# Other layout and other steps for the stacks, the maxima and the loads of an attention kernel, and an output projection of 14 products

## The chip, the cores and the metric

One core of a Trainium2 chip runs the whole kernel. The metric is the device time of one execution in microseconds; three executions of the kernel before took 717.62, 720.45 and 721.08 us, median 720.45. Less is better. The core has five engines with queues of their own that work in order: TensorE (PE, with its weight loads as PEld), VectorE (DVE), ScalarE (ACT), GpSimd (POOL) and SyncE (SP), which here only issues transfers (DMA). The profile's lines are those of the kernel before.

## What is computed

Two parts that share nothing are computed and set side by side: `a`, an attention with memory, and `b`, a filter in the frequency domain.

```python
# a: S=2048 rows, D=576, H=32 heads of 18, N=4 segments of 512 rows
for s in range(4):
    logits = qs @ ks.T * scale + mask          # causal, within the segment
    a_dot  = softmax(logits) @ vs
    a_mem  = (phi(qs) @ M) / (phi(qs) @ z + 1e-6)     # phi(t): t+1 if t>0, else exp(t)
    o      = g * a_mem + (1 - g) * a_dot       # g = sigmoid(beta), one per head
    M += phi(ks).T @ vs;  z += phi(ks).sum()
a = concat(o) @ wo
# b:
b = irfft2(rfft2(x) * (w_r + 1j * w_i))
```

## The kernel before, in words

Everything is kept near float32 by splitting: a float32 number becomes two (`fp32r`) or three (`bf16`) parts, and a product becomes a sum of products of parts.

The time line has four stages. First the forward transform of `b` (`FFT.forward`). Then the projections (`ATT.projections`): for each of four segments nine tiles of 128 columns of Q and K (`qk_unit`, four of Q, one that is half Q and half K, four of K) and four of V (`v_unit`), with the middle of the transform taken in between. Each tile of Q and K is split into three bf16 parts (`sp3`) and stored in DRAM (`qkD`); phi of Q is stored too (`pqD`), phi of K is transposed on TensorE (`ptr`) and copied to `pk` for the memory. Third comes the inverse transform, into which `prologue` weaves the start of attention. Last comes attention proper, a loop over `t` with one head of one segment per step, 128 heads and 5 steps to run out.

The work is in order by hand (`manual_schedule`): generators emit instructions, and the loop in `attention` says which generator goes on at which place of a step. `hh` is `t` modulo 4, a group `k` has four heads, a stack `n` has two groups. In step `t`:

- `s1(t+10)` computes the scores of the head ten ahead, in three accumulations, and takes their row maxima on DVE. For two of the three (`red`) DVE adds the causal mask itself (L641, then a read of its accumulator); in the other the mask comes by a product with a triangle (`tri`, L646).
- `mpath(k+2)` turns four heads' maxima into rows of the stack Q: it gathers them (L659, L660), splits them in two on GpSimd (`mh`, L662, L663), transposes them on TensorE (L666), copies them (`mts`, L669), and two steps later ACT's queue sends them into rows 108 and 109 of Q (L672). It begins at `hh==1` and goes on at `hh==3`.
- `s2(t)` computes the transposed scores with the maxima already subtracted (L682 to L691, 110 rows: 108 of the stack and 2 of the maxima) and ACT takes the exponentials; at `hh==3` GpSimd cuts the triangles of four heads (L696).
- `pv` multiplies with V (L711), `pv_out` and `u_dmas` store the result (`U`, `uD`, `rD`).
- `run_bg(1.2)` advances the background by 1.2 steps per head: `mixed`, which combines segment `g-1` (`combine`: `ux` and `pb` to `am`, then the parts `oh` and `ol`, L819 and L832) and begins the memory term of segment `g` (`mem1`); `den`, the denominators of the next segment (L765, it reads `pq`, which `mem1` loads); and `oproj`, the output projection of segment `g-1` (L849).
- Transfers wait in lists `q` and `qu` and are issued two per step on SP's queue; `later(k, f)` puts one some steps off.

A stack has 108 rows of 8 heads by 512: six pairs of bf16 parts of Q and K by 18 numbers of a head. `stack_dmas` loads it in six transfers of 18 rows; each row is gathered from eight pieces of 1 KB, since `qkD` has one row per column of the weights with three parts of 1 KB behind one another. Stacks for Q are three in turn, for K four.

`oproj` has for each of four blocks of 128 rows and two halves of 288 columns an accumulation of 15 products: five tiles of rows (four of 126, one of 72) times three pairs of parts (`oh` with `woh`, `oh` with `wol`, `ol` with `woh`). The last segment goes through `last_proj` instead.

Of the kernel before, what the change touches and what calls it, by code (L numbers as in the profile page):

```python
# [340 lines left out]
BF=mybir.dt.bfloat16  # L341
H=32; DH=18; SC=float(DH)**-0.5
# [41 lines left out]
class ATT:  # L384
    def __init__(s,nc,tc,io,cp,dp):
# [6 lines left out]
        s.qkD=[d(f"qkD{i}",[1152,3,512],BF) for i in range(4)]  # L392
# [68 lines left out]
    def qk_unit(s,g,mt,tp,pp):  # L461
# [9 lines left out]
        nc.scalar.copy(sp3[:,0],ps)  # L471
# [6 lines left out]
        nc.vector.tensor_tensor(ps,ps,sp3[:,0],op=OP.subtract)  # L478
# [3 lines left out]
        nc.scalar.copy(sp3[:,1],ps)  # L482
        yield
        nc.tensor.matmul(ps,s.nid,sp3[:,1],start=False,stop=True,skip_group_check=True)
        nc.scalar.copy(sp3[:,2],ps)
        nc.sync.dma_start(s.qkD[g][128*mt:128*mt+128],sp3)
# [3 lines left out]
        n=r1-k0; c0=128*mt+k0-576  # L490
# [4 lines left out]
        nc.scalar.copy(s.pk[:,:,c0:c0+n],pt[:,:,:n])  # L495
# [99 lines left out]
    def late_setup(s,cp):  # L595
# [3 lines left out]
        s.woh=cp.tile([126,5,576],F32R,name="woh",bufs=1); s.wol=cp.tile([126,5,576],F32R,name="wol",bufs=1)  # L599
        for t in range(6):  # L600
            if t>1: yield
            if t<5:
                x=cp.tile([128,576],F32,name="ob")[:126]; q.append(x)
                nc.sync.dma_start(x,io["wo"][:,576*t:576*t+576])
            for _ in range(2): yield
            if t>0:
                x=q.pop(0)
                nc.scalar.copy(s.woh[:,t-1],x)
                nc.gpsimd.tensor_tensor(s.wol[:,t-1],x,s.woh[:,t-1].bitcast(F32),op=OP.subtract)
        yield  # L610
        yield from s.gates()
    def stack_dmas(s,n,qk):

        nc=s.nc; g,G=divmod(n,4)
        L=[]
        T,base,order=((s.Qs[n%3],0,(0,0,0,1,1,2)),(s.Ks[n%4],576,(0,1,2,0,1,0)))[qk]
        for pc,o in enumerate(order):
            a=s.qkD[g][base+8*G*18:base+8*G*18+18,o]
            ap=bass.AP(tensor=a.tensor,offset=a.offset,ap=[[1536,18],[1536*18,8],[1,512]])
            def go(T=T,pc=pc,ap=ap):  # L620
                nc.sync.dma_start(T[18*pc:18*pc+18],ap)
                if pc==5: s.loaded.add((n,qk))
            L.append(go)
        return L
# [5 lines left out]
    def s1(s,t):  # L630
# [163 lines left out]
    def mixed(s,g):  # L794
# [3 lines left out]
        for i in range(5+d):  # L798
            next(c,None); yield
            if i>=d:  # L800
                for _ in s.mem1(g,i-d): yield
# [4 lines left out]
    def combine(s,g):  # L806
# [6 lines left out]
        def high(u):  # L813
            r=126 if u<4 else 72
            s.oh[u]=tp.tile([126,512],F32R,name="oh",bufs=5); s.ol[u]=tp.tile([126,512],F32R,name="ol",bufs=5)
            (nc.vector.tensor_copy if s.now>=119 else nc.scalar.copy)(s.oh[u][:r],s.am[u][:r])
        def low(u):
            r=126 if u<4 else 72
            eng().tensor_tensor(s.ol[u][:r],s.am[u][:r],s.oh[u][:r].bitcast(F32),op=OP.subtract)  # L819
        late=g==2  # L820
        for t in range(7+late):
            if t>1 and not late: high(t-2); low(t-2)
            if t<5:
                r=126 if t<4 else 72; x=xs[t]
# [8 lines left out]
                if t<2: s.later(1,lambda t=t: s.ux_load(g,t+3))  # L833
            if late and 1<t<7: high(t-2)
            if late and t>2: low(t-3)
            yield
    def oproj(s,g):
        nc=s.nc
        oh,ol=s.oh,s.ol
        for tb in range(4):  # L840
            ob=s.tp.tile([128,576],F32,name="ob")
            c=slice(128*tb,128*tb+128)
            for hf in range(2):
                ps=(s.ps.tile([128,512],F32,name="po",tag=s.potag) if s.potag else s.post("po"))[:,:288]
                w=slice(288*hf,288*hf+288)
                L=[(a,b,t) for a,b in ((oh,s.woh),(oh,s.wol),(ol,s.woh)) for t in range(5)]
                for i,(a,b,t) in enumerate(L):
                    r=126 if t<4 else 72
                    nc.tensor.matmul(ps,a[t][:r,c],b[:r,t,w],start=i==0,stop=i==14)  # L849
                    if i==7: yield  # L850
# [41 lines left out]
    def prologue(s):  # L892
# [7 lines left out]
        for t in range(10):  # L900
# [223 lines left out]
```

## Time and profile before

| | before |
|---|---|
| three executions, us | 717.62, 720.45, 721.08 (median 720.45) |
| the profiled execution, us | 718.92 |
| its span, first to last instruction, us | 717.2 |
| granted TensorE clock, mean | 0.997 |
| instructions | 14460 |
| DMA packets, under 2 KB of them | 83304, 50750 |

The profile shows one execution. Busy time of an engine is the time in which it works on at least one instruction; a window counts it in a stretch of the span. A wait names the engine and line that waited, and what ended the wait. The chain follows back from the last instruction to whatever released each step. The attention loop runs from about 355 to 680 us, the projections from about 75 to 275 us, the inverse transform between them.

### The profile page before, as it was taken

To read this page: it belongs to the slowest core of one execution; us is meant where nothing else is said; L and a number is where in the kernel's file an instruction comes from. 1 tells how busy PE (TensorE), PEld (TensorE's weight loads), DVE (VectorE), ACT (ScalarE), POOL (GpSimd) and SP (SyncE) were. 2 spreads that over 40 slices of the span, in tenths; PEclk is the share of its full clock that TensorE was granted. 3 is DMA by queue.
4 is the path that set the end of the run, shared out by engine and by line. 5 is a ranking of instruction groups with operands and counts; after the bars stand their busy time and mean duration, and the time that the engine had idled before them with its cause. 6 is when DMAs were issued, how large, how long until landed. Compare 5 with 4: busy or idle time off the path is not lost. (4 is left out here: it accounts for less than half of the span.)

```text
span 717.2 us, 14460 instructions
## 1 busy us (share of the span) xinstructions
PE 684.1 (95%) x5007; PEld 505.7 (71%) x5007; DVE 552.3 (77%) x1270; ACT 450.1 (63%) x985; POOL 211.1 (29%) x403
## 2 busy tenths in 40 slices
PE   4999999999999999999999899899999999999997
PEld 4988869879779879999854444444466445664497
DVE  5999979899699789788588787878466876568633
ACT  3665796585586575444487677767466776567521
POOL 5432000100200111665154333435123662235300
PEclk9999999999999999999999999999999999999999
DMA  8995435645363568899547665776446775441152
GB/s 305 293 280 164 148 118 185 192 169 182 110 220 147 178 198 281 208 231 228 165 111 174 171 172 136 185 173 170 114 126 158 195 169 126 126 137 42 28 153 83
DMA packets 83304, 121.02 MB, mean 169 GB/s; under 512 B 11472, under 2 KB 50750, under 8 KB 83096
## 3 DMA queue, kind: packets, MB, share of 16 engines
q1 hardware_dynamic: 76580, 104.11, 50.3%
q0 software_dynamic: 5632, 15.76, 8.0%
q8 instruction: 39, 0.64, 0.4%
q10 hardware_dynamic: 1020, 0.25, 0.2%
q14 instruction: 33, 0.27, 0.1%
HBM read 81.78 MB, written 38.24 MB: 167 GB/s over the span
## 5 line engine op out<-in xcount | busy, mean ns | idle before, releaser
L641 DVE CUSTOM_DVE_ANT_0 junk<-s,x 128x512 bf16<-128x512 f32 (+1 forms) x256 | 141.4, 552 | 67.2 <-PE s L637 62.0
L696 POOL TENSOR_SCALAR_AFFINE_SELECT P<-P 128x512 f32<-128x512 f32 (+2 forms) x132 | 78.8, 623 | 67.3 <-ACT P L683 51.8
L647 DVE TENSOR_REDUCE mx<-s 128x4 f32<-128x512 f32 x128 | 87.7, 686 | 2.9 <-PE s L646 0.7
L683 ACT ACTIVATE P<-s 128x512 f32<-128x512 f32 x128 | 76.4, 597 | 16.5 <-PE s L682 5.4
L711 PE MATMUL pv<-P,vs 128*32 128x512 f32 (+3 forms) x1024 | 82.8, 441 | 0.0
L692 ACT ACTIVATE P<-s 128x256 f32<-128x256 f32 x128 | 49.4, 386 | 49.7 <-PE s L691 49.6
L688 ACT ACTIVATE P<-s 128x512 f32<-128x512 f32 x128 | 76.1, 594 | 2.0 <-PE s L687 1.8
L637 PE MATMUL s<-Ks,Qs 108*128 108x384 bf16 (+3 forms) x256 | 69.1, 301 | 1.2 <-DVE mx L647 0.9
L711 PEld LDWEIGHTS pv<-P,vs 128*32 128x32 f32 x1024 | 27.2, 109 | 45.3 <-issue 42.5
L459 PE MATMUL pj<-x,wqkh 128*128 128x512 f32 x162 | 56.5, 409 | 0.0
L205 DVE TENSOR_TENSOR Z<-t,t 128x290 f32<-128x290 f32 (+1 forms) x96 | 48.4, 554 | 0.1
L637 PEld LDWEIGHTS <-Qs 108*128 108x128 bf16 x320 | 31.5, 98 | 22.6 <-issue 11.3
L506 POOL MEMSET vt<- 128x32 f32 x16 | 2.4, 166 | 149.1 <-PE pm L516 127.7
L205 DVE TENSOR_TENSOR t<-Z 128x580 f32<-128x580 f32 x64 | 46.0, 755 | 0.0
L142 PE MATMUL f<-ftab,eh 128*128 128x290 f32 (+1 forms) x160 | 32.5, 322 | 12.1 <-DMA ftab<-ftab 9.5
L646 PE MATMUL s<-tri,idb 128*128 128x128 bf16 x256 | 43.2, 220 | 0.0
L295 PE MATMUL i<-civ,Y 128*128 128x256 f32 (+1 forms) x288 | 39.0, 288 | 0.2 <-POOL Y L280 0.2
L295 PEld LDWEIGHTS i<-civ,Y 128*128 128x128 f32 (+1 forms) x288 | 36.4, 181 | 1.0 <-POOL Y L280 0.4
L306 PE MATMUL i<-itab,T 128*128 128x290 f32 (+1 forms) x224 | 36.3, 305 | 0.1
L637 PE MATMUL s<-Ks,x 108*128 108x384 bf16 (+3 forms) x128 | 35.3, 306 | 1.1 <-DVE mx L647 0.6
L142 PEld LDWEIGHTS f<-ftab,eh 128*128 128x128 f32 (+1 forms) x160 | 26.2, 207 | 14.1 <-issue 8.5
L459 PE MATMUL pj<-x,wqkl 128*128 128x512 f32 x90 | 35.5, 395 | 0.0
(203 smaller groups left out, 1820.8 us busy)
## 6 DMA issues: line engine op xcount, KB each, us to landing
qkD<-sp SPq DMA_DIRECT2D x36, 384.0 KB
Ks<-qkD SPq DMA_DIRECT2D x72, 144.0 KB
x<-qkD SPq DMA_DIRECT2D x60, 144.0 KB
Qs<-qkD SPq DMA_DIRECT2D x60, 144.0 KB
xin<-xb SPq DMA_DIRECT2D x16, 384.0 KB
cfw<-cfw POOLq DMA_DIRECT2D x16, 384.0 KB, 4.4
civ<-civ POOLq DMA_DIRECT2D x16, 384.0 KB, 7.6
vs<-vD SPq DMA_DIRECT2D x16, 330.0 KB
```

The costliest lines, as they stand in the source:

```text
L142: nc.tensor.matmul(p[:,r,:FP],x,t,start=n==0,stop=n==6)
L205: v.tensor_tensor(o,a,b,op=op)
L295: nc.tensor.matmul(p[:m,k],Y[i][:,q,c*128:c*128+m],cc[:,hl,o:o+256],start=n==0,stop=n==5)
L459: s.nc.tensor.matmul(out,a,b,start=i==0,stop=i==len(L)-1)
L637: nc.tensor.matmul(out,Q[:108,h,128*i:128*i+128],K[:108,h,:128*(i+1)],start=True,stop=True)
L641: nc.vector.tensor_tensor_reduce(out=junk[:,:w],in0=src,in1=s.mask[:,512-w:],scale=1.0,scalar=-3.0e38, op0=OP.add,op1=OP.max,accum_out=s.m ...
L647: nc.vector.tensor_reduce(out=s.mx[k][:,hh],in_=pa.rearrange("p (b c) -> p b c",c=128),axis=mybir.AxisListType.X,op=OP.max)
L683: nc.scalar.activation(P[0][:,hh],p0,AF.Exp,scale=SC)
L688: nc.scalar.activation(P[1][:,hh],p1,AF.Exp,scale=SC)
L692: nc.scalar.activation(P[2][:,hh],p2,AF.Exp,scale=SC)
L696: nc.gpsimd.affine_select(out=x[:,r],in_=x[:,r],pattern=[[0,r.stop-r.start],[1,128]],compare_op=OP.is_ge,fill=0.0,base=0,channel_multiplie ...
L711: nc.tensor.matmul(s.pvt[32*hh:32*hh+32,128*j:],vt[:,j,19*h:19*h+32],mv[0][:,hh,mv[1]],start=j==0,stop=j>1,skip_group_check=True)
```

## The change

1. *Stacks.* The columns of the weights of Q and K are put in another order on the host: tiles 0 to 3 hold the first 16 numbers of 8 heads of Q each, the middle tile the last two numbers of all heads of Q and of K, tiles 5 to 8 those of K like Q. `qkD` gets one block per tile with the parts outermost, so that eight heads of one number and one part are 8 KB in a row; K's parts are stored in reversed order. The middle tile goes to `reD`, with parts repeated, in six stores. A stack is loaded by four transfers of 48, 32, 16 and 12 rows of 8 KB. `pqD` and `pk` keep their old order, so their stores and copies go by steps.
2. *Maxima.* `s1` works on the head eleven ahead (the prologue does one head more), and `mpath` begins at `hh==0` and goes on at `hh==1`. For heads 11 to 14 all three accumulations get the triangle by a product, and DVE a plain reduction.
3. *Loads and background.* The three loads of `ux` move into the wait of the reciprocals, three to five heads earlier. Four steps of `oproj` go ahead of `den`. The five tiles of a segment are taken in the order 4, 0, 1, 2, 3.
4. *Projection.* For segments 0 to 2 the fifth tile's three products become two: rows 72 to 127 of `oh` and rows 72 to 87 of `ol` for that tile are filled, by three transfers within SBUF, with copies of parts, and `woh` and `wol` get matching rows from a sixth load of `wo`.

```diff
+ORD=(4,0,1,2,3)
...
 def host_wo(w):
-    o=np.zeros((126,5,D),np.float32)
-    o[:,:4]=w[:504].reshape(4,126,D).transpose(1,0,2)
-    o[:72,4]=w[504:]
+    o=np.zeros((128,6,D),np.float32)
+    o[:126,:4]=w[:504].reshape(4,126,D).transpose(1,0,2)
+    o[:72,4]=w[504:]; o[72:,4]=w[504:560]; o[72:88,5]=w[560:]
...
-        s.qkD=[d(f"qkD{i}",[1152,3,512],BF) for i in range(4)]
+        s.qkD=[d(f"qkD{i}",[8,3,128,512],BF) for i in range(4)]
+        s.reD=[d(f"reD{i}",[24,32,512],BF) for i in range(4)]
...
-        if qr>r0: nc.sync.dma_start(s.pqD[g][128*mt:128*mt+qr],e[:qr])
+        if qr>r0:
+            a=s.pqD[g][0]
+            J=[(18*8*mt*512,[[512,16],[18*512,8]],e[:qr])] if mt<4 else [((16+j)*512,[[18*512,32]],e[32*j:32*j+32]) for j in range(2)]
+            for o,ap,x in J: nc.sync.dma_start(bass.AP(tensor=a.tensor,offset=a.offset+o,ap=ap+[[1,512]]),x)
...
-        nc.sync.dma_start(s.qkD[g][128*mt:128*mt+128],sp3)
+        if mt!=4: nc.sync.dma_start(s.qkD[g][mt-(mt>4)].rearrange("i p c -> p i c"),sp3)
+        else:
+            for r,i,c,n in ((0,0,1,3),(0,1,1,2),(0,2,1,1),(64,0,3,3),(64,0,2,2),(64,0,1,1)):
+                m={3:0,2:3,1:5}[n]; a=s.reD[g][r*12//64+2*m]
+                x=sp3[r:r+64,i:i+c] if c==n else sp3[r:r+64,i:i+1].to_broadcast([64,n,512])
+                nc.sync.dma_start(bass.AP(tensor=a.tensor,offset=a.offset,ap=[[512,64],[64*512,n],[1,512]]),x)
...
-        nc.scalar.copy(s.pk[:,:,c0:c0+n],pt[:,:,:n])
+        pk=s.pk.rearrange("p a (h d) -> p a h d",d=18)
+        if mt==4: nc.scalar.copy(pk[:,:,:,16:],pt[:,:,:n].rearrange("p a (d h) -> p a h d",d=2))
+        else: nc.scalar.copy(pk[:,:,8*mt-40:8*mt-32,:16],pt.rearrange("p a (d h) -> p a h d",h=8))
...
-        T,base,order=((s.Qs[n%3],0,(0,0,0,1,1,2)),(s.Ks[n%4],576,(0,1,2,0,1,0)))[qk]
-        for pc,o in enumerate(order):
-            a=s.qkD[g][base+8*G*18:base+8*G*18+18,o]
-            ap=bass.AP(tensor=a.tensor,offset=a.offset,ap=[[1536,18],[1536*18,8],[1,512]])
-            def go(T=T,pc=pc,ap=ap):
-                nc.sync.dma_start(T[18*pc:18*pc+18],ap)
...
+        T=(s.Qs[n%3],s.Ks[n%4])[qk]
+        u=G+4*qk
+        for p0,i0,i1 in ((0,0,3),(48,qk,2+qk),(80,2*qk,1+2*qk)):
+            L.append(lambda p0=p0,i0=i0,i1=i1: nc.sync.dma_start(T[p0:p0+16*(i1-i0)].rearrange("p a c -> p (a c)"),s.qkD[g][u,i0:i1].rearrange("i (d h) c -> (i d) (h c)",h=8)))
+        def go():
+            nc.sync.dma_start(T[96:108],s.reD[g][12*qk:12*qk+12,8*G:8*G+8])
...
+            if 11<=t<15:
+                nc.tensor.matmul(src[:,w-128:w],s.idb,s.tri,start=False,stop=True,skip_group_check=True)
+                nc.vector.tensor_reduce(out=s.mg[k][:,hh,i:i+1],in_=src,axis=mybir.AxisListType.X,op=OP.max)
+                return
...
+            A,B=s.oh[u],s.ol[u]
+            l=B if u<4 else tp.tile([128,512],F32R,name="ol4",bufs=1)
+            eng().tensor_tensor(l[:r],s.am[u][:r],A[:r].bitcast(F32),op=OP.subtract)
+            if u==4:
+                s.later(1,lambda: nc.sync.dma_start(B[:72].bitcast(F32),A[:72].bitcast(F32)))
+                s.later(2,lambda: (nc.sync.dma_start(A[72:128].bitcast(F32),l[:56].bitcast(F32)),nc.sync.dma_start(B[72:88].bitcast(F32),l[56:72].bitcast(F32))))
...
-                L=[(a,b,t) for a,b in ((oh,s.woh),(oh,s.wol),(ol,s.woh)) for t in range(5)]
...
+                L=[(a,b,t,126) for a,b in ((oh,s.woh),(oh,s.wol),(ol,s.woh)) for t in range(4)]+[(oh,s.woh,4,128),(ol,s.wol,4,88)]
...
-        for t in range(10):
+        for t in range(11):
...
+                        if 2<i<6: s.ux_load(g-1,ORD[i-3])
                         next(r); yield
-                    for u in range(3): s.ux_load(g-1,u)
                     yield from r
                     bg.append(s.mixed(g))
-                    if g<3: bg.append(s.den(g+1,lane))
-                    bg.append(s.oproj(g-1))
+                    o=s.oproj(g-1)
+                    if g<3: bg.append(itertools.islice(o,4)); bg.append(s.den(g+1,lane))
+                    bg.append(o)
...
-            a=s.s1(t+10) if t+10<128 else iter(())
+            a=s.s1(t+11) if t+11<128 else iter(())
...
-            if hh==3 and m is not None: steps(m,1)
+            if hh==1 and m is not None: steps(m,1)
             steps(b,1)
-            if hh==3 and m is not None: steps(m,1)
-            if hh==1 and k+2<32: m=s.mpath(k+2); next(m)
+            if hh==1 and m is not None: steps(m,1)
+            if hh==0 and k+2<32: m=s.mpath(k+2); next(m)
```

More of the change, by code (lines that the diff above doesn't have):

```diff
@@ L832, in combine @@
                     eng().tensor_tensor(s.am[t][:r],x[:r],s.am[t][:r],op=OP.add)
[L833 to L835 removed]
+                t=i
+                if t<2: s.later(1,lambda t=t: s.ux_load(g,ORD[t+3]))
+            if late and 1<t<7: high(ORD[t-2])
+            if late and t>2: low(ORD[t-3])
             yield
```

71 lines of the change are left out of this document (38 added, 33 removed).

## The prediction

> **What bounds the kernel now.** I read the page's busy times first, then the stage windows, then TensorE's waits in the attention stage, and the chain last. The page's first part, one profiled execution:
>
> ```profile
> PE 684.1 (95%) x5007; PEld 505.7 (71%) x5007; DVE 552.3 (77%) x1270; ACT 450.1 (63%) x985; POOL 211.1 (29%) x403
> ```
>
> TensorE is busy nearly throughout. Whether it is the limit is read per stage; three windows (columns: stretch, length, busy time of PE, weight load, DVE, ACT and POOL, granted clock, DMA share, GB/s):
>
> ```profile
> 140.00:180.00 40.00, 40.00 (x243) 34.55 (x242) 37.27 (x68) 28.57 (x57) 0.35 (x4) 1.00 0.57 190
> 300.00:340.00 40.00, 40.00 (x321) 37.53 (x320) 34.34 (x86) 17.61 (x44) 23.00 (x35) 1.00 0.92 228
> 415.50:423.50 8.00, 8.00 (x76) 4.14 (x74) 6.94 (x22) 6.13 (x17) 2.88 (x7) 1.00 0.68 183
> ```
>
> The projections (first), the inverse transform with its prologue (second) and four undisturbed heads of attention (third) leave TensorE no gap; DVE and ACT have one to two microseconds over in eight. So time is won by fewer products or shorter waits of TensorE, and lost by new waits of it. The waits there are, from 355 to 680 us (total us, times, longest):
>
> ```profile
> PE s L682 <- DMA Qs<-mts: 3.2, 3, 1.4
> PE pd L765 <- DMA pq<-pqD: 1.4, 1, 1.4
> PE pb L826 <- DMA rr<-rrD: 1.2, 1, 1.2
> PE s L637 <- DMA Qs<-qkD: 0.4, 1, 0.4
> PE s L682 <- DMA x<-mts: 0.2, 1, 0.2
> ```
>
> All five end on a transfer, 6.4 us together. The chain (start, length, what) tells how long these transfers take and what the products of the output projection cost:
>
> ```profile
> 372.67 7.55 DMA Qs<-mts
> ...
> 401.24 5.59 DMA x<-mts
> ...
> 458.87 0.68 SPq L805
> 459.61 0.38 SPq L805
> 460.03 0.48 SPq L805
> 460.61 5.79 DMA rr<-rrD
> 466.44 0.38 PE pb L826
> ...
> 481.35 8.42 DMA Qs<-mts
> ...
> 500.58 6.41 DMA pq<-pqD
> ...
> 512.28 1.25 PE po L849 x8
> ...
> 693.37 2.93 PE po L849 x22
> ```
>
> **Products of the output projection.** 22 products in 2.93 us are 0.133 us each. Segments 0 to 2 have 8 accumulations each (four blocks of rows, two halves); each loses one of 15: 24 x 0.133 = **-3.2 us**, all on the path, since TensorE is the limit there.
>
> **Maxima eleven heads ahead.** The transfer of the maxima (mts) was issued three heads before its first use, some 6 us at 8.00 us for four heads, and lands 5.6 to 8.4 us after issue (chain): hence the waits. It is issued two heads earlier now, five heads or 10 us ahead, more than the longest landing. Both mts rows go: **-3.4 us**. What is late next is the transposition of the maxima, which now follows their making by one head instead of two; TensorE takes its work in order, so it and all behind it would wait. One head's worth of rows in the undisturbed stretch:
>
> ```profile
> 415.04 0.63 POOL L696 TENSOR_SCALAR_AFFINE_SELECT P<-P 128x512 f32<-128x512 f32 x1
> ...
> 415.39 0.27 PE L637 MATMUL s<-x,Qs 108*128 108x256 bf16 x1
> ...
> 416.72 0.08 DVE L641 DVE_READ_ACCUMULATOR2_ANT mg<- 128x1 f32 x1
> ...
> 418.13 0.28 PE L637 MATMUL s<-x,Qs 108*128 108x256 bf16 x1
> ...
> 418.53 0.22 PE L646 MATMUL s<-tri,idb 128*128 128x128 bf16 x1
> ...
> 418.59 0.22 PE L637 MATMUL s<-Ks,Qs 108*128 108x128 bf16 x1
> ...
> 418.80 0.08 DVE L641 DVE_READ_ACCUMULATOR2_ANT mg<- 128x1 f32 x1
> ...
> 419.44 0.22 POOL L663 TENSOR_TENSOR mh<-mg,mh 128x16 bf16<-128x16 f32 x1
> ...
> 422.19 0.22 PE L666 MATMUL mt<-idb,mh 128*128 128x128 bf16 x1
> ```
>
> Before: the last maximum at 418.80, its two halves done on GpSimd at 419.66, 0.86 us later; transposed at 422.19, 2.5 us to spare. After: the last maximum of a group falls one head earlier, like that at 416.72, so the halves are done at 417.58, and TensorE asks for them right behind the product at 418.13: 0.7 us to spare. GpSimd also takes its work in order:
>
> ```profile
> L819 POOL TENSOR_TENSOR ol<-am,oh 126x512 fp32r<-126x512 f32 (+1 forms) x10 | 12.7, 1270 | 16.4 <-ACT oh L816 15.4 <-PE pn L784 1.0
> L832 POOL TENSOR_TENSOR am<-ux,am 126x512 f32<-126x512 f32 (+1 forms) x8 | 10.1, 1273 | 4.5 <-DVE ux L831 3.3 <-PE s L682 1.2
> ```
>
> Where one of these 18 stands in front, TensorE waits 1.27 - 0.7, about 0.6 us. A transposition comes in every fourth head, so some four or five are hit; the first one or two come while DVE is still catching up: **+1.5 us** for about 30 transpositions, ends 0 and 11 (18 x 0.6). I take the low part, because the combining steps that issue the 18 also lengthen TensorE's own heads. GpSimd's selects, the only other work of size there, end before that place (the last at 415.67). The other instructions of the step (a reduction on DVE, two small copies on ACT, the issue on ACT's queue) move along, their number unchanged; ACT has the time, as 6.13 of 8 us show.
>
> The eight accumulations of heads 11 to 14 that get the triangle by a product cost one product of 128 columns each, 0.06 us (418.53 to 418.59): **+0.5 us**; DVE saves its 0.08 us of reading the accumulator each time, which I count as nothing. The eleventh head in the prologue moves one head's score products from one stage bound by TensorE to another: 0.
>
> **Loads at other steps.** The three loads of ux stood on SP's queue right before rr (458.87 to 460.61, 1.7 us), and TensorE waited 1.2 us for rr. They go three to five heads earlier: **-1.2 us**; rr is then not late. Four steps of the output projection now stand between the last load of pq (issued at 500.58, landed 6.41 us later) and the denominators that read it. Each step holds seven products, four take over three heads, more than 6.4 us: **-1.4 us**. A window on each side of that wait (columns as above):
>
> ```profile
> 504.50:508.00 3.50, 2.08 (x13) 0.35 (x5) 1.26 (x3) 1.32 (x3) 0.41 (x2) 1.00 0.62 146
> 508.00:511.50 3.50, 3.50 (x19) 1.59 (x22) 1.82 (x5) 2.12 (x4) 0.83 (x2) 0.52 0.48 131
> ```
>
> After the window with the wait, the granted clock is 0.52 for 3.5 us: 3.5 x 0.48 = **-1.7 us** more, which go with the wait. [...]
>
> **Stacks.** Four transfers instead of six, on the page:
>
> ```profile
> Ks<-qkD SPq DMA_DIRECT2D x72, 144.0 KB
> Qs<-qkD SPq DMA_DIRECT2D x60, 144.0 KB
> ```
>
> The bytes stay, the issues fall from 192 to 128. A row of 8 KB isn't in this trace; its ends are the wait it could remove, **-0.4 us** (Qs<-qkD above), and the same wait again if it lands later. I take the first: fewer issues stand in front. Otherwise loads are hidden by a whole group's heads (16 us). If that cover went, each of 13 later Q stacks would show as the 0.4 did, +5 us.
>
> What pays for it lies in the projections: the store of qkD in pieces of 1 KB, five more stores for each middle tile, one more of pqD, columns of pk written in another order. All stores are SP's and nobody on TensorE waits for them within its 3.5 us per tile; no stack is read before the projections of segment 3, and then it is one of segment 0. The copy to pk reads PSUM in steps of eight elements. Nearest rows:
>
> ```profile
> L495 ACT COPY pk<-ptr x15: 357/588/622, 100.5 to 225.5; 128x512 f32<-128x512 f32 x12, 128x256 f32<-128x256 f32 x3
> PE pj L484 <- ACT sp L482: 1.9, 3, 1.0
> ```
>
> Between no change and the slowest elementwise row of that width (1.27 us, GpSimd above) it costs ACT 0 to 10 us in all; ACT has about 11 us over in 40 there, but in segment 0 TensorE already waits for ACT (second row, 1.0 us at most). So 0 on the path, with up to 3.4 us (five copies x 0.68) as upper end.
>
> The three copies from SBUF to SBUF per segment make SP wait for GpSimd's 1.27 us; behind them stand stack loads with heads to spare. They are read by the last two products of an accumulation, some 46 us after the combining begins (466.44 to 512.28): 0, and if that cover went, a landing of 6 to 8 us, once per segment. That the tile of 72 rows is combined first changes no count: 0. The sixth load and copy of wo fall in segment 0, on ACT: 0.
>
> **Sum.** -3.2 - 3.4 + 1.5 + 0.5 - 1.2 - 1.4 - 1.7 - 0.4 = **-9.3 us**. The profiled execution took 718.92 us (span 717.2), so 709.6 by its own time. It is 1.5 us faster than the median of the three runs, 720.45; from that median it is **711.1 us**.
>
> **Rivals.**
> 1. *The transposition becomes the wait (slower).* If GpSimd's selects slip behind the making of the maxima, so that a 1.27 us operation or two selects of 0.63 stand in front every time, each of 30 transpositions costs 0.6 us or more; at 0.5 us each the 15 us eat the gain (10.8 without its own term) and more, at 0.8 us it is 720.45 - 10.8 + 24 = 734. For it: only 0.7 us to spare. Against it: GpSimd is busy 2.88 of 8 us. Deciding point against half a percent: 14.4/30 = 0.48 us.
> 2. *The waits turn up elsewhere (no change).* ACT (6.13) and DVE (6.94 of 8.00) use the pauses to catch up; without them TensorE waits for them instead. Only the products count: 720.45 - 3.2 + 0.5 = 717.8. For it: DVE's 87%. Against it: the undisturbed stretch runs at full pace.
> 3. *The maxima still land late.* Rows of 8 KB ahead of small pieces lengthen their landing beyond 10 us: 711.1 + 3.4 = 714.5. The longest landing seen is 8.42.
> 4. *The strided copy delays the projections*: 711.1 + 3.4 = 714.5. [...]
> 5. *More waits go* (those of DVE at the start of attention, of ACT on earlier mts transfers): up to 6 us more, 705.
>
> **How the numbers follow.** Forecast 0.55, rival 1 0.08, rival 2 0.11, rival 3 0.10, rival 4 0.08, rival 5 0.08. Half a percent, 3.6 us, is what a measurement tells from no change: below 716.8 is faster. Faster 0.81 (forecast and rivals 3, 4, 5), same 0.11 (rival 2), slower 0.08 (rival 1). The range takes in rivals 3, 4 and most of 2 and 5: 705.5 to 718.5.
>
> **What would show it.** Output products 24 fewer; no wait of L682 on mts, none of pd on pq, none of pb on rr; no window at half clock near 508 us; a small new wait of the transposition. Wrong would be: a wait of the transposition in most groups, mts landing over 10 us, L484 waiting for ACT for several microseconds, or a copy to pk over 1.2 us.

## The result: no change that can be told

The changed kernel took 718.77 us (median of 22 runs, 715.25 to 724.88), the kernel before, on the same chip, 719.89 us (714.56 to 728.79): a ratio of 0.9994, interval 0.9975 to 1.0013. The prediction was 711.1 us, with a range of 705.5 to 718.5. (Ratios here and below are formed from undisturbed runs, medians from all that are listed, so the two need not divide out exactly.) The profiled execution of the changed kernel took 717.86 us, its span 716.2 us, 1.0 us less than before.

The busy times, from the first part of the page of the changed kernel:

```profile
PE 681.5 (95%) x4991; PEld 501.8 (70%) x4991; DVE 551.0 (77%) x1262; ACT 450.6 (63%) x986; POOL 210.0 (29%) x403
```

TensorE has 2.6 us less to do and executes 16 products fewer (5007 before): 24 output products go, eight triangle products come. That part of the change is there. TensorE's waits in the same stretch, 355 to 680 us (total us, times, longest), changed kernel:

```profile
PE s L653 <- ACT mts L689: 3.5, 3, 2.6
PE s L702 <- ACT P L703: 3.4, 9, 1.1
PE mt L686 <- POOL mh L683: 2.2, 5, 0.8
PE s L653 <- DVE mx L667: 1.2, 2, 1.0
PE po L874 <- DVE am L806: 0.7, 1, 0.7
```

In this kernel L653 is the first score product (L637 before), L702 the first product of the second scores (L682), L686 the transposition of the maxima (L666), L689 ACT's copy of them to mts (L669) and L692 their transfer (L672), L703 the exponential (L683), L874 the output product (L849). All five waits on transfers are gone: none for mts at L702, none of pd for pq, none of pb for rr, none for a stack at the scores. In their place TensorE waits for ACT (two rows, 6.9 us) and for GpSimd (2.2 us). Before, it waited for GpSimd nowhere and for ACT little:

```profile
PE s L682 <- ACT P L683: 1.3, 4, 0.4
```

The longest new wait, in the chain of the changed kernel between 396.5 and 407 us (start, length, what):

```profile
390.35 7.16 DMA Qs<-reD
...
397.59 8.78 DMA x<-mts
...
406.39 0.26 ACT mts L689
406.65 0.04 issue
406.69 0.27 PE s L653
```

and what TensorE does in it and just behind it (stretch, length, busy time of PE, granted clock, DMA share, GB/s):

```profile
404.12:406.69 2.57, 0.00 (x0) 1.00 0.87 214
406.69:410.20 3.51, 3.51 (x26) 0.67 0.19 68
```

The lines fit together. The transfer of one group's maxima is issued at 397.59 and lands 8.78 us later. There is one buffer mts, so ACT's copy of the next group's maxima cannot start before that landing. The copy frees the PSUM tile that the next score product needs, so TensorE stands for 2.57 us. Behind it the granted clock is half from 407.86 to 411.28 us, of which the second window holds the larger part; all of it costs 3.41 x 0.5 = 1.7 us. ACT's own waits for the buffer in this kernel, from its waits (columns as above):

```profile
ACT mts L689 <- DMA x<-mts: 3.8, 2, 2.8
ACT mts L689 <- DMA Qs<-mts: 0.4, 1, 0.4
```

Before the change this wait existed too, 2.6 us in all, but TensorE was then held up by the same transfers at the use of the maxima:

```profile
ACT mts L669 <- DMA Qs<-mts: 2.6, 3, 1.3
```

### The profile page after: what moved, and what is told of

Its sections match the earlier page's. It is cut to its first block, busy times and chain, and to the rows that moved or that the text cites. A ratio compares the mean times of both kernels' runs of the same rounds, so it can differ in the third digit from the quotient of the medians.

```text
span 716.2 us, 14406 instructions
## 1 busy us (share of the span) xinstructions
PE 681.5 (95%) x4991; PEld 501.8 (70%) x4991; DVE 551.0 (77%) x1262; ACT 450.6 (63%) x986; POOL 210.0 (29%) x403
## 4 chain that ended last, share of the span: by engine, by line
PE 62%; DMA 12%; ACT 4%; DVE 3%; issue 3%; POOL 3%; SPq 1%; ACTq 0%; POOLq 0%; DVEq 0%
PE pj L461 12%; PE pjv L461 8%; PE s L653 8%; PE pv L731 7%; PE po L874 4%; PE i L306 3%; PE i L295 3%; PE s L702 3%; DMA x<-mts 2%; DMA yb<-yout 2%; PE s L706 2%; PE pn L804 2%; PE pm L529 2%; PE s L666 1%; PE s L711 1%
## 5 line engine op out<-in xcount | busy, mean ns | idle before, releaser
L661 DVE CUSTOM_DVE_ANT_0 junk<-s,x 128x512 bf16<-128x512 f32 x248 | 137.0, 552 | 64.2 <-PE s L653 59.6
L703 ACT ACTIVATE P<-s 128x512 f32<-128x512 f32 x128 | 77.7, 607 | 16.6 <-PE s L666 5.2
L708 ACT ACTIVATE P<-s 128x512 f32<-128x512 f32 x128 | 77.5, 605 | 2.6 <-PE s L707 2.4
L712 ACT ACTIVATE P<-s 128x256 f32<-128x256 f32 x128 | 49.9, 389 | 44.2 <-PE s L711 44.1
L653 PE MATMUL s<-Ks,Qs 108*128 108x384 bf16 (+3 forms) x256 | 69.0, 301 | 2.1 <-DVE mx L667 1.2
L653 PEld LDWEIGHTS <-Qs 108*128 108x128 bf16 x320 | 31.6, 99 | 23.5 <-issue 12.1
L666 PE MATMUL s<-tri,idb 128*128 128x128 bf16 x256 | 43.1, 220 | 0.0
L461 PE MATMUL pj<-xh,wqkl 128*128 128x512 f32 x90 | 35.5, 395 | 0.0
```

What stands on the lines that cost most here:

```text
L461: s.nc.tensor.matmul(out,a,b,start=i==0,stop=i==len(L)-1)
L653: nc.tensor.matmul(out,Q[:108,h,128*i:128*i+128],K[:108,h,:128*(i+1)],start=True,stop=True)
L661: nc.vector.tensor_tensor_reduce(out=junk[:,:w],in0=src,in1=s.mask[:,512-w:],scale=1.0,scalar=-3.0e38, op0=OP.add,op1=OP.max,accum_out=s.m ...
L703: nc.scalar.activation(P[0][:,hh],p0,AF.Exp,scale=SC)
L708: nc.scalar.activation(P[1][:,hh],p1,AF.Exp,scale=SC)
```

## The experiments

**Theory 1, "given back":** the gains that the prediction counted are real, and the wait for the single buffer (with what follows from it) eats them. **Theory 2, "nothing to gain":** the waits for transfers were only the places where ACT and VectorE caught up. Eighteen kernels were run; they are told in seven groups.

### The buffer: with the change and without it

```diff
-        mt=s.sm.tile([32,128],BF,name="mts",bufs=1)
+        mt=s.sm.tile([32,128],BF,name="mts",bufs=2)
```

This line alone, in the changed kernel:

> The changed kernel with two buffers instead of one for the copied maxima (mts). Theory 1 (given back): the gains of the change are real, but the 8 KB rows delay the small transfer of the maxima in every second group, ACT's next copy of maxima waits for it in the single buffer, and TensorE waits behind ACT. Then TensorE's wait for the copy (3.5 us in the changed kernel) and the half clock after it (about 1.6 us) go: 5 us, some 714 us, 0.993 of before. Theory 2 (nothing to gain): the waits of before were only the places where ACT and DVE caught up; ACT's wait for the buffer turns up as waits for the exponentials, and the time stays at 0.999 of before.

Measured: 713.71 us (711.80 to 714.22, 6 runs), ratio 0.9894 (0.9859 to 0.9929). TensorE's waits:

```profile
PE s L702 <- ACT P L703: 4.2, 10, 1.2
PE mt L686 <- POOL mh L683: 2.7, 6, 0.8
PE s L653 <- DMA x<-qkD: 1.0, 1, 1.0
```

The wait for the copy is gone, and so is the half clock within the attention stage: the granted clock is 1.00 in each of four windows of 80 us from 356 to 676 us, where the changed kernel has 0.98 in the first. The same line in the kernel before:

> The kernel before with a second buffer for the transposed maxima (mts), nothing else. Theory 1 (the wait for the single buffer is new with the change; the gains of the change are real and the wait ate them): in the kernel before, ACT waited for that buffer 2.6 us in all, while TensorE stood at the same transfers anyway, so the buffer alone is worth at most 2 us: ratio to the kernel before 0.997 to 1.001, and the changed kernel with two buffers (0.989) owes most of its gain to the change. Rival (the buffer is a gain of its own and the change adds nothing): ratio 0.989 to 0.992, the same as the changed kernel with two buffers.

Measured: 720.32 us, ratio 1.000 (0.9962 to 1.0038). So the buffer is worth nothing without the change and 5.1 us with it (718.77 less 713.71; by the two ratios, each against the kernel before as it ran beside it, 7.2): the change did win time, and the buffer took it back. For the change as a whole Theory 2 falls.

### The parts alone

The stacks alone (`stack_dmas`, `qk_unit` and the host's order of columns from the changed kernel):

> The kernel before with the new stacks alone (order of columns, stores, four transfers in rows of 8 KB). Theory 1: every second transfer of maxima lands in 5 to 8 us instead of 4, the other in 1.5 to 2.5; with a lead of three heads, 6 us, the waits of L682 on the maxima stay or grow from 3.4 us to about 6: 1.000 to 1.006. Theory 2: the maxima are no limit, 1.000 with waits of before's size. If the strided copy to pk costs ACT much, L484 (here under its own line) waits for ACT more than 2 us in the projections.

Measured: 724.35 us, ratio 1.0034 (1.0001 to 1.0068). TensorE waits for mts as before (2.0 + 1.3 us) and 1.8 us for rr. No gain, rather a small loss; of the two landing times that were expected in turn, see the last section.

The maxima alone, with the old six loads for each stack:

```diff
-            a=s.s1(t+10) if t+10<128 else iter(())
+            a=s.s1(t+11) if t+11<128 else iter(())
...
-            if hh==3 and m is not None: steps(m,1)
+            if hh==1 and m is not None: steps(m,1)
```

> The kernel before with the maxima eleven heads ahead and their earlier steps alone; stacks still in rows of 1 KB. Theory 1: TensorE's wait of L682 on the maxima (3.4 us) goes; the transposition waits for GpSimd 2 to 3 us; the copy of the maxima waits little, since with pieces of 1 KB no maxima land later than 7.6 us: 0 to -1.5 us, 0.999. Theory 2: 1.000, and waits of TensorE for ACT's exponentials in place of those on the maxima.

Measured: 728.21 us, ratio 1.0108 (1.0068 to 1.0148), which neither theory had. Its first waits:

```profile
PE s L637 <- DMA x<-qkD: 4.6, 2, 2.6
PE s L637 <- DMA Qs<-qkD: 4.4, 3, 3.7
```

One head more of lead needs the stack one head sooner, and with six loads it is not there: 9.0 us of waits in place of 0.4. The two parts belong together. The prediction asked for the transposition what it needs sooner, and did not ask it for the score products.

The loads at other steps alone:

> The kernel before with the part 'loads at other steps' alone: the ux loads three to five heads earlier, and four steps of the output projection ahead of the denominators. The prediction's terms are 1.2 us (rr), 1.4 us (pq) and 1.7 us (half clock behind the wait for pq), together 4.3 us: ratio 0.994. Theory 1 (each part's terms are real, but parts alone shift where small transfers meet large ones): the waits for rr and pq go, the ratio lies between 0.994 and 1.002, and what is missing is found in waits for mts or stacks. Theory 2 (the waits were only the places where ACT and VectorE caught up): the waits for rr and pq go, and waits for ACT's exponentials or VectorE's maxima of some 2.6 us come in their place: ratio 0.998 to 1.000.

Measured: 717.18 us, ratio 0.9968 (0.9935 to 1.0002): some 2.3 us of the 4.3, with an interval that just takes in no change. The waits for rr and pq are gone; waits for mts stay (3.1 us), the one for ACT's exponentials grows from 1.3 to 3.4 us, and a stretch of half clock lies elsewhere, from 457.5 to 460.9 us (0.98 in the mean from 436 to 516 us).

The 14 products alone (new layout of the last tile, sixth load of wo, three copies from SBUF to SBUF for each segment, tile of 72 rows first):

> The kernel before with the output projection of 14 products alone (and the order 4, 0, 1, 2, 3 of tiles it needs). Theory 1: the 16 products of segments 0 and 1 are worth 2.1 us; the 8 of segment 2 lie at the end, beside the chain of transfers of the last segment, and are worth 0 to 1 us: 0.996 of before, and in the trace TensorE has new pauses between 685 and 702 us. Theory 2: 1.000, the same products missing but the pauses spread over the attention loop.

Measured: 725.51 us, ratio 1.0054 (1.0016 to 1.0093): slower, where a gain was expected of every theory. This miss is taken up below.

### Products and transposition within the mended kernel

15 products again, with two buffers:

> The changed kernel with a second mts buffer and 15 products for each accumulation again in all segments (old layout of the last tile, no copies from SBUF to SBUF, no sixth load of wo). Against the changed kernel with two buffers (713.7 us). The prediction's term: 24 x 0.133 = 3.2 us slower, 716.9. With the reading that the 8 accumulations of segment 2 lie in the tail beside the chain of transfers of the last segment and are worth nothing: 16 x 0.133 = 2.1 us slower, 715.8. If the 14 products cost more than they save, as the kernel before with them alone (ratio 1.005) could mean: at or below 713.7.

Measured: 716.01 us, ratio 0.9960 (0.9929 to 0.9991). That is 2.3 us slower than with 14 (713.71) by the medians and 4.8 by the two ratios, whose intervals touch. The 2.1 us of 16 products and the 3.2 of 24 are both near that, so the time doesn't tell them apart. The traces do so for the other eight: they lie behind the last group of attention, and from the last product of the second scores to the end of the span it is 42.8 us with 15 products and 43.4 with 14, both with two buffers. There the chain of the changed kernel goes through transfers of the last segment:

```profile
680.59 1.91 DMA rD<-U
682.90 4.97 DMA ux<-uD
...
697.26 4.23 DMA rd<-rrD
```

and TensorE has new waits, from 680 us on, here in the changed kernel:

```profile
PE pb L883 <- DVE ux L884: 1.1, 1, 1.1
PE po L874 <- ACT ob L876: 0.4, 1, 0.4
PE pb L883 <- DMA rd<-rrD: 0.3, 1, 0.3
```

Fewer products there only let TensorE wait sooner: from the same product to the end it is 43.2 us before and 44.2 us after the change.

The transposition one head later, with two buffers:

```diff
-            if hh==1 and m is not None: steps(m,1)
+            if hh==2 and m is not None: steps(m,1)
```

> The changed kernel with a second mts buffer and the transposition of the maxima one head later, four heads ahead of the first use instead of five. Against the changed kernel with two buffers (713.7 us, where TensorE waited 2.7 us for GpSimd at the transposition, six times). Theory 1 (that wait is a cost of its own): the wait goes, 711 us. Rival (the landing needs the fifth head): TensorE waits for mts at the first use, 2 us or more come back, 713 to 716 us.

Measured: 718.72 us, ratio 0.9981 (0.9949 to 1.0013), 5 us slower. The wait of the transposition for GpSimd is gone, no wait for mts came; both expectations missed. Instead:

```profile
PE s L653 <- DVE mg L661: 4.9, 18, 0.3
PE s L702 <- ACT P L703: 2.9, 5, 1.8
```

The score products wait 18 times for VectorE's maxima, 0.3 us each. Why the later transposition brings VectorE into the way isn't settled here.

### ACT's other wait: the issue itself

With two buffers, TensorE still waited 4.2 us for ACT's exponentials. In several of these kernels ACT stands still just ahead of issuing the maxima's transfer, and what ends the pause is the landing of a load that has nothing to do with the maxima. In the kernel with 15 products and two buffers (ACT's waits; L700 is the exponential there):

```profile
ACT P L700 <- DMA Qs<-reD: 4.1, 1, 4.1
```

Which load it is can be counted. In the chain of the changed kernel quoted first, the issue at 397.59 follows the landing of the load issued at 390.35. SP's issues in that stretch (start, length, what, count):

```profile
390.35 0.39 SPq L637 DMA_DIRECT2D Qs<-reD  x1
390.78 0.36 SPq L776 DMA_DIRECT2D pq<-pqD  x1
391.19 0.84 SPq L635 DMA_DIRECT2D Ks<-qkD  x2
393.31 0.31 SPq L776 DMA_DIRECT2D pq<-pqD  x1
394.76 0.30 SPq L635 DMA_DIRECT2D Ks<-qkD  x1
395.57 0.30 SPq L637 DMA_DIRECT2D Ks<-reD  x1
396.66 0.31 SPq L776 DMA_DIRECT2D pq<-pqD  x1
```

Seven issues lie between, so the maxima's transfer is the eighth after that load. The same count holds for the 4.1 us pause above and for a 3.0 us pause in the kernel with the later transposition. The traces also hold the semaphores, the counters by which a landing is reported, and they show whose rule this is: this program uses eight for the transfers of these two queues, nearly always in turn (in the changed kernel 518 of 534 transfers have the semaphore of the eighth before), and in all three cases the instruction just ahead of the issue waits for the semaphore that the transfer itself uses. So a transfer here is mostly issued when the eighth one before it has landed. On SP this costs nothing that shows. On ACT the exponentials stand behind it. Added up over the 30 issues (from the end of ACT's instruction before to the issue), ACT stood 1.6 us in the kernel before, 5.6 after the change, 7.1 with two buffers and 10.7 with 14 products alone. So the issue was moved to another queue:

```diff
-        else: s.later(2,lambda: nc.scalar.dma_start(out,mt))
+        else: s.later(2,lambda: nc.gpsimd.dma_start(out,mt))
```

Changed kernel, two buffers, GpSimd's queue:

> The changed kernel with a second mts buffer, and the transfer of the maxima issued from GpSimd's queue instead of ACT's. In the traces so far ACT stood still just ahead of this issue, until the eighth transfer issued before it (any of the loads of SP) had landed: 1.6 us in all before the change, 5.6 after it, 7.1 with two buffers, 10.7 in the kernel before with 14 products alone. Theory 1b (each issue waits for the eighth one before it, and on ACT the exponentials stand behind that wait): TensorE's wait for ACT's exponentials at the first product of the second scores (4.2 us with two buffers) goes, ACT is also rid of 30 issues of 0.62 us, and the time falls from 713.7 to 708 to 711 us. Rival (ACT's pauses are only where it caught up, or GpSimd's 0.66 us for each issue delays the halves of the maxima and the selects as much): 713 to 717 us, with the wait of the transposition for GpSimd above its 2.7 us.

Measured: 709.60 us (708.89 to 710.05, 5 runs), ratio 0.9848 (0.9807 to 0.9890). TensorE's waits:

```profile
PE mt L686 <- POOL mh L683: 2.5, 6, 0.8
PE s L653 <- DVE mx L667: 1.2, 2, 1.0
PE s L702 <- ACT P L703: 0.7, 3, 0.3
```

As expected: the wait for the exponentials falls from 4.2 to 0.7 us, the wait for GpSimd doesn't grow, 4.1 us go by the medians (3.3 by the ratios, whose intervals overlap a little). With SP's queue instead:

> The changed kernel with a second mts buffer, and the transfer of the maxima issued from SP's queue. ACT is free of the wait and of the issue as with GpSimd, GpSimd has nothing more to do, but the transfer stands behind the loads on SP's queue, which waits 2 to 9 us at a time for buffers. Theory 1b with cover enough (five heads, about 10 us): 708 to 711 us. If the queue of SP delays it past its use: TensorE waits for mts at the first product of the second scores for several microseconds, 714 to 725 us.

Measured: 711.05 us, ratio 0.9875 (0.9838 to 0.9913); the wait for the exponentials is 0.7 us here too, and none for mts. What both runs have in common is that ACT no longer issues. They free ACT of the wait and of 30 issues of 0.62 us together; the two were not told apart.

The control, the kernel before with two buffers and GpSimd's queue:

> The kernel before with a second mts buffer (which alone gave a ratio of 1.000) and the transfer of the maxima issued from GpSimd's queue: the control for the two others. Theory 1b: ACT's pauses ahead of the issue were 1.6 us (6.0 with two buffers), and the waits for the landing (3.4 us) stay: 716 to 719 us, ratio 0.995 to 0.999. Rival (the queue is what the time hangs on, with the change or without): ratio 0.990 or below.

Measured: 716.43 us, ratio 0.9943 (0.9915 to 0.9970). The queue is worth some 4 us there as well; the waits for mts (1.9 us) and rr (0.8 us) stay. Between this kernel and the one at 709.60 us lies the change alone: 6.8 us, of 9.3 predicted. Under ACT's queue, with two buffers, it is 6.6 (720.32 less 713.71), so what the change is worth doesn't hang on the queue.

Only one of the two remedies, the queue without the buffer:

> The changed kernel with the transfer of the maxima issued from GpSimd's queue, but the single mts buffer. With both remedies it took 709.6 us, with the buffer alone 713.7, unmended 718.8. If the two costs add up (buffer 5 us, queue 4 us): about 714.7 us, with ACT still waiting for the buffer at the copy of the maxima. If the wait for the buffer was only the consequence of ACT's late issue: 709 to 711 us.

Measured: 716.73 us, ratio 0.9944 (0.9915 to 0.9973), with a larger wait for the copy than in the changed kernel (3.5 us):

```profile
PE s L653 <- ACT mts L689: 6.1, 5, 1.8
```

So the wait for the buffer isn't a consequence of ACT's late issue. Both remedies are needed: by the medians 2.0 us by the queue alone, 5.1 by the buffer alone, 9.2 by both; by the ratios 3.6, 7.2 and 10.5, so that there the two add up.

### Stacks and maxima together

> The kernel before with the new stacks, the maxima eleven heads ahead and a second mts buffer: the parts 'stacks' and 'maxima' together, without the loads at other steps and without the 14 products. Alone, the stacks gave 1.003 and the maxima 1.011. The prediction's terms for the pair: -3.4 + 1.5 + 0.5 - 0.4 = -1.8 us. If the parts need each other and the buffer: 717 to 719 us, with no wait for mts at the first use. If the gain of the changed kernel with two buffers comes from the other parts: 720 us or more.

Measured: 721.01 us, ratio 1.0005 (0.9979 to 1.0031): no gain, against the expectation that they only need each other and the buffer. The wait for mts at the first use is gone, but ACT stood 10.1 us ahead of its issues in this kernel, and TensorE waits 4.0 us for the exponentials, 2.1 for GpSimd at the transposition, 1.9 for a load of a stack and 1.4 for rr. By the expectation's other branch the gain of the changed kernel with two buffers comes from the other parts, or only together with them: with two buffers and ACT's queue the pair stands at 1.0005, with the loads at other steps as well at 0.9960 (the kernel with 15 products), and with the 14 products at 0.9894. That the pair would pay with another queue wasn't tried.

### Why the 14 products alone cost time

First with ACT's wait taken away:

> The kernel before with 14 products for each accumulation, a second mts buffer and the transfer of the maxima issued from GpSimd's queue. The 14 products alone made it slower (ratio 1.005), with 10.7 us of ACT standing ahead of that issue. Theory 1b (the sixth load of wo and the copies from SBUF to SBUF only shifted which transfer stands eighth ahead of the maxima's): without that wait the products pay, about 2 us below the same kernel with 15 products and this queue. Rival (the added loads and copies cost TensorE time by themselves): 2 to 5 us above it.

Measured: 725.18 us, ratio 1.0063 (1.0029 to 1.0096). A miss: 8.8 us above the same kernel with 15 products (716.43), more than the rival had, so ACT's pauses were not the reason. TensorE waits for transfers again, and more than in the kernel with this queue and 15 products (1.9 us for mts, no wait for pq):

```profile
PE s L686 <- DMA Qs<-mts: 5.6, 2, 3.3
PE pd L769 <- DMA pq<-pqD: 3.6, 2, 2.2
```

Then its pieces, the sixth load of wo alone:

> The kernel before with the sixth load of wo and its copy in the first segment alone (new order of the loads, 15 products as before, no copies from SBUF to SBUF). In the kernel with 14 products alone the loss of 6 us arose at heads 16 to 32, ahead of any output projection. If the sixth load delays the landing of the maxima there (three heads ahead in this kernel): 723 to 727 us, the loss at heads 16 to 32 and TensorE waiting 3 us or more for mts. If the loss came from somewhere else: 719 to 721 us.

Measured: 720.16 us, ratio 0.9998 (0.9972 to 1.0024). Not that one. Then 14 products without the copies from SBUF to SBUF:

```diff
-            if u==4:
-                s.later(1,lambda: nc.sync.dma_start(B[:72].bitcast(F32),A[:72].bitcast(F32)))
-                s.later(2,lambda: (nc.sync.dma_start(A[72:128].bitcast(F32),l[:56].bitcast(F32)),nc.sync.dma_start(B[72:88].bitcast(F32),l[56:72].bitcast(F32))))
...
-                L=[...]+[(oh,s.woh,4,128),(ol,s.wol,4,88)]
+                L=[...]+[(oh,s.woh,4,72),(ol,s.wol,4,72)]
```

> The kernel before with 14 products and all that goes with them except the three copies from SBUF to SBUF in each segment; the last two products of an accumulation read 72 rows, so the last tile lacks its two low-order terms. If the copies are what costs (they stand on SP's queue, wait there for GpSimd, and each holds up the loads of pq and ux behind it): the products pay, 716 to 719 us. If not: 723 to 727 us, as with the copies (725.5).

Measured: 719.50 us, ratio 0.9968 (0.9933 to 1.0003): between the two ranges, nearer the first, and no gain that is clear. And the order of the tiles alone:

> The kernel before with 15 products, where only the order of the five tiles is changed: the tile of 72 rows first in the loads of pq and ux, the denominators and the combining. The prediction counted this at 0. If the order is what costs (the first loads of pq and the first denominators come for other rows, and TensorE waits longer for pq): 723 to 727 us, with more than 3 us of waits for pq and the half clock behind them. If not: 719 to 721 us.

Measured: 721.66 us, ratio 1.0022 (0.9989 to 1.0055). So by the times of twelve executions each the copies cost 6.0 us in the kernel before (725.51 less 719.50); neither load nor order can be told from nothing. The traces don't bear it out. In the one with the copies the stretch from the first head's exponentials to the 32nd's takes 72.6 us, where the kernel before takes 65.6, and the first copy is issued only behind it, at 485.5 us; from there to the last head it is 250.9 us against 251.7. The trace without copies, of a long execution (span 723.1 us), takes 70.7 us for the first stretch too. So what the 14 products cost alone, and why, stays open; in the changed kernel with two buffers, with their copies, they pay (2.3 to 4.8 us, above).

### The transposition behind one more product

```diff
-            if hh==1 and m is not None: steps(m,1)
             steps(b,1)
-            if hh==1 and m is not None: steps(m,1)
+            if hh==1 and m is not None: steps(m,2)
```

in the kernel with two buffers and GpSimd's queue:

> The changed kernel with two mts buffers, the issue on GpSimd's queue, and the transposition of the maxima behind the last product of the second scores of its head instead of ahead of it, some 0.3 us later. TensorE waited 2.5 us for GpSimd at the transposition, six times, at most 0.8. If that wait is a cost of its own: 1 to 2 us go, 707.5 to 708.5 us. If it only gave DVE time that TensorE would have to wait for elsewhere: 709.6 us, with new waits of the score products for DVE.

Measured: 708.17 us (706.36 to 713.25, 6 runs), ratio 0.9802 (0.9766 to 0.9838). The wait shrinks (the trace is of the longest of the six executions, 713.25 us):

```profile
PE mt L686 <- POOL mh L683: 1.6, 4, 0.7
```

This is the fastest kernel of the study, 12 us below the kernel before; its distance to the one at 709.60 us is within the two intervals, so whether the wait of 2.5 us is a cost of its own isn't decided.

## Where the prediction was right and where it was wrong

**Reading of the bound: right in the main.** TensorE limits the attention stage, and the five waits on transfers all went. The list of waits was not whole, though: in the same window TensorE also waited for engines, 1.5 us for VectorE's maxima and 1.3 us for ACT's exponentials being the largest, and the second grew to 3.4 us.

**Maxima, -3.4 us: the step that failed.** The two rows on mts went, as counted. But the prediction moved the transposition, ACT's copy and the transfer and wrote that they "move along, their number unchanged; ACT has the time". It counted ACT's busy time and put at nothing what ACT must wait for: the landing of the previous transfer, because mts is a single buffer. Its lead of five heads, 10 us, is the time to the use. The buffer is wanted again three heads after the issue, by the next group's copy (the issue comes one head behind its own copy, since `later` counts from the step before): in these traces 5.6 us after it at the least before the change and 5.8 after, and the prediction itself had landings of 5.6 to 8.4 us. The wait stood in the trace of before (2.6 us) and was not looked at, because TensorE was waiting at the same moments. Measured in its place: 3.5 us of waits of TensorE for the copy and 1.7 us of half clock behind the longest, and 5.1 us of time that a second buffer gives back. With two buffers in both kernels the change is worth 6.6 us, not 1.1.

ACT's other wait, for the eighth transfer before its issue, grew from 1.6 to 5.6 us with the change, and the prediction didn't see it either. Moving the issue is worth some 4 us, but with the change and without it, so it isn't what keeps the whole from its 9.3 us. It may be what keeps the maxima from theirs: stacks and maxima alone, with two buffers and ACT's queue, gained nothing (1.0005) where the terms gave -1.8 us.

**Transposition, +1.5 us: near in size, mostly by other causes.** 2.2 us in five waits of at most 0.8 (2.7 in six with two buffers), within the ends of 0 and 11; whether they are time lost isn't decided. The prediction had combining steps of 1.27 us in front, in four or five groups, and the selects out of the way. In the changed kernel one wait (0.43 us) is behind a combining step; the longest (0.76) is behind a step of 1.41 us that splits `wo`, two (0.40 each) behind selects, and the first (0.24) behind none. The size is luck in part. Rival 1, a wait in every group, did not come.

**Output products, -3.2 us: a third not on the path.** 2.3 us by the medians in the kernel with two buffers, 4.8 by the ratios, which leaves the size open. Eight of the 24 lie in the tail, which got no shorter without them, since transfers set the end there. The prediction put "all on the path" for all three segments, "since TensorE is the limit there".

**Copies from SBUF to SBUF, 0: right at most beside the other parts.** In the kernel before they cost 6.0 us by the times, and no trace shows where.

**Loads at other steps, -1.2 - 1.4 - 1.7 us: mechanism right, size partly.** Both waits went, the half clock near 508 us too (1.00 from 500 to 520 us in the changed kernel). Alone the part gave some 2.3 us of 4.3, with another pause and another half clock elsewhere; in the changed kernel the half clock follows the pause at 404 us.

**Stacks, -0.4 us:** the wait went in the changed kernel; alone the new stacks gave no gain (1.0034). What they do is to let the maxima be made a head earlier.

**Projections, 0: right.** The copy to pk in steps of eight elements takes 596 ns at the median, where the straight one took 588, and TensorE's wait for ACT there is 2.0 us where it was 1.9:

```profile
L508 ACT COPY pk<-ptr x12: 572/596/629, 103.4 to 225.0; 128x512 f32<-128x512 f32 x12
PE pj L490 <- ACT sp L488: 2.0, 3, 1.0
```

Rival 4 is out: the strided read of PSUM by ACT shows no more here than these 8 ns, and 26 ns in the three copies of the middle tiles (401 ns at the median against 375).

**The rivals.** What came about gives the result of rival 2 (no change) by another mechanism. Rival 2 had ACT and VectorE catch up in the pauses; what the second buffer gave back is a wait that ACT was made to do. Of ACT's part in the waits for the exponentials it is not known: the other queues took its wait and 30 issues off it together. Rival 3 (maxima land late) has part of the truth: the longest landing was 8.78 us, below the 10 us of lead, so the use was not late, but the buffer was. Rival 5 did not come: the waits for VectorE's maxima were 1.2 us where they had been 1.5.

## What to carry to other kernels

When a transfer is moved earlier, ask not only when its data is used but when its source buffer is wanted again, and by which engine; a wait that is hidden behind another wait of the same trace can become the wait when that one is removed (here ACT's 2.6 us for mts before, TensorE's 3.5 us for ACT's copy after). Issue small transfers from an engine that nobody waits for: an issue can stand behind the landing of unrelated transfers, and everything in that engine's order stands with it (here 4.1 us in the kernel with 15 products and two buffers, with the exponentials behind it). Test parts of a change together with what they need: here two parts alone made the kernel slower, the buffer alone did nothing, and change, buffer and queue together took 10 us.

## What the runs showed of the hardware that was not expected

The landing of a small transfer varied fivefold at one size. The 8 KB of one group's maxima took between 1.5 and 8.0 us from issue to the end of the last packet in the changed kernel (median 2.3; the 8.0 is the transfer of 8.78 us in the chain, which counts up to what the landing released), mostly short and long in turn from group to group; before the change between 1.5 and 7.6 (median 4.3). That the loads with rows of 8 KB make the long ones long isn't shown: with the new stacks alone it was 1.5 to 7.6 us (median 3.7), at the longest about what it was before, and short and long in turn only in places.

TensorE's granted clock was half behind some pauses and not behind others of about the same length. In the trace of before a pause of 1.42 us (505.71 to 507.13 us) was followed by a clock of 0.50 from 508.1 to 511.5 us, in that of the changed kernel one of 2.57 us (404.12 to 406.69 us) by 0.50 from 407.86 to 411.28 us. But behind a pause of 1.40 us in the same trace of before (396.49 to 397.88 us) the clock stayed at 1.00. In the kernel with GpSimd's queue and two buffers no wait of TensorE in the attention stage is above 1.0 us, and the granted clock is 1.00 in all nine windows of 20 us from 356 to 536 us. What decides it is not shown here.

The scatter between executions is larger than most terms here: 714.56 to 728.79 us in 22 runs of the kernel before, 708.89 to 710.05 us in 5 runs of the one with two buffers and GpSimd's queue. That it goes with the waits for transfers isn't shown: the fastest kernel has few of them too and ran from 706.36 to 713.25 us in 6 runs. In the trace of its longest execution TensorE waits 1.8 us for VectorE in the inverse transform, ahead of the attention stage. A single profile places a loss of a few microseconds only for its own execution.
